# Dealing out PSUM in single-bank tiles in the first two phases of a transformer block's forward and backward pass

## Chip, cores, metric

One core of one Trainium2 chip. The metric is the device time of one execution in microseconds (us), the median of several runs. "The profile" is one profiled execution; its time axis starts with the span. Its records of matmuls can be a few per cent short, so counts of matmuls are rough.

## The reference, cut to what matters

A pre-layernorm block: attention over 8 keys at distance 0, 2, ... 14 (32 heads of 16), then an FFN with gelu, and the gradients of all of it for a given `grad_out`. S = 2048 tokens, D = 512, F = 1792, bf16.

```python
h  = x + attention(layernorm(x), wqkv, wo)      # 8 keys per token, dilation 2
h2 = h + gelu(layernorm(h) @ w1 + b1) @ w2 + b2
out, vjp = jax.vjp(h2_of, x, wqkv, wo, w1, b1, w2, b2)
return out, *vjp(grad_out)
```

## The kernel before

Three phases. Phase 1 is the attention forward pass by chunks of 512 tokens. Phase 2 is the FFN forward and backward, also by chunks. A handover joins them, in which chunk 3 finishes its attention while the FFN of chunk 0 starts. Phase 3 is the attention backward pass with the weight gradients. Instructions of phases 1 and 2 are put in order by a scheduler when the kernel is built, those of phase 3 by hand. These are the parts that the change and the argument touch:

```python
psY = pool("psY", 2, space=PSUM)       # 2 banks: Y(name) = one bank, 512 fp32
psT = pool("psT", 2, space=PSUM)       # 2 banks: transpositions
psX = pool("psX", 2, space=PSUM)       # 2 pairs of banks
def X(name):
    return psX.tile([P, 2, 512], F32, name=name, tag="x")
# ... phase 1: q, k, v and logits in X; ps_sum, ps_r, ps_wo and ps_band in Y

def p2_h(c):                           # first FFN matmul and gelu, chunk c
    for (f0, f1) in FB:                # blocks of 4, 4, 4, 2 slices of F
        # ... xb, xa: rings of 2 buffers
        for fp in range(f0, f1, 2):
            ps = X("ps_h")
            for i in range(2):
                # ... 4 matmuls into ps[:, i, :]
                A.activation(out=xb[...], in_=ps[:, i, :], func=ACT.Identity, bias=...)
                A.activation(out=x2[...], in_=ps[:, i, :], func=ACT.Square, bias=...)   # x2 is in xa
        gt, dt_ = block_tiles()        # ring of 5 blocks
        # ... eight DVE steps on xb, xa: gt = gelu, the last writes dt_ = gelu'
        tok_store(gt, f0, f1, gT_d, c) # transposition by DMA (SP queue), then a store (POOL)

def p2_rest(c):
    goT = ft("goT")
    SY.dma_start_transpose(out=goT[:], in_=gof[c * CH:(c + 1) * CH, :])
    # ...
    for j in range(TPC):               # FFN output: 16 matmuls per tile, read by ACT
        ps = Y("ps_f2")
    for bi, (f0, f1) in enumerate(FB):
        for fp in range(f0, f1, 2):
            ps = X("ps_gg")
            for i in range(2):
                # ... 4 matmuls w2T x goT into ps[:, i, :]
                # DVE: dt *= ps[:, i, :], with row sums (gb1p)
        tok_store(dts[bi], f0, f1, ghT_d, c)
    for j in range(TPC):               # gradient of the layernorm's output, read by ACT
        ps = Y("ps_gl2")
# ...
ms = tc.manual_schedule()              # phase 3 from here
ms.__enter__()
V.memset(glf[:, :, S:SP], 0.0)
```

A round of phase 2 has two parts. In the *section*, PE runs the 56 ps_gg matmuls of chunk c, its 56 ps_gl2 matmuls and some ps_h of chunk c+1. In the *FFN-output half*, it runs ps_f2 and the other ps_h of chunk c+1.

Of the kernel before, what the change touches and what calls it, by code (L numbers as in the profile page):

```python
# [36 lines left out]
def kernel(  # L37
# [57 lines left out]
    psX = pool("psX", 2, space=bass.MemoryType.PSUM)  # L95

    def X(name):
        return psX.tile([P, 2, 512], F32, name=name, tag="x")
# [157 lines left out]
    def dots(wp, ql, kw_, L, mask):  # L256
        for g in range(4):
            pr = wp.tile([P, W, 512], BF16, name="pr", tag="prod", bufs=2 + (wp is not late))
            V.tensor_tensor(out=pr[:], in0=ql[:, g, :].unsqueeze(1).to_broadcast([P, W, 512]),  # L259
                            in1=_sub(kw_[:, g, PAD:PAD + 512], [[-DIL, W], [1, 512]]), op=ALU.mult)  # L260
            for hf in range(2):
                for w4 in range(4):
                    T.matmul(L[32 * w4:32 * w4 + 32, hf, :], lhsT=Emat[:, g, :], rhs=pr[:, 2 * w4 + hf, :],
                             start=(g == 0), stop=(g == 3), skip_group_check=True)
        if mask:
            for hf in range(2):
                T.matmul(L[:, hf, 0:16], lhsT=mk[:, hf].rearrange("p a b -> p (a b)"), rhs=ident[0:16, 0:16],
                         start=False, stop=True, skip_group_check=True)
# [97 lines left out]
    def p1_proj(c, sel, dst, off):  # L366
        for g2 in range(2):
            ps = X("ps_qkv")
            for gg in range(2):
                g = 2 * g2 + gg  # L370
                for dc in range(DC):
                    T.matmul(ps[:, gg, :], lhsT=wqkv[:, dc, sel * D + g * P:sel * D + (g + 1) * P],  # L372
                             rhs=st_[c]["ln1T"][:, dc, :], start=(dc == 0), stop=(dc == DC - 1))
            A.copy(out=dst[:, 2 * g2:2 * g2 + 2, off:off + CH], in_=ps[:])  # L374
# [25 lines left out]
    def p1_dots(c):  # L400
        d = st_[c]
        d["L"] = X("ps_L")
        dots(late, d["qt"], d["kt"], d["L"], c == 0)

    def p1_sm1(c):
# [3 lines left out]
        A.copy(out=asb[:], in_=L[:, 0, :])  # L409
        m1 = late.tile([P, 512], BF16, name="m1", tag="m1", bufs=1)  # L410
        V.tensor_tensor(out=m1[:], in0=asb[:], in1=L[:, 1, :], op=ALU.max)
# [8 lines left out]
        for hf in range(2):  # L420
            T.matmul(L[:, hf, :], lhsT=nSum4[0:32, :], rhs=m3[:], start=False, stop=True, skip_group_check=True)
        e = late.tile([P, 2, 512], BF16, name="e", tag="e", bufs=1)
        A.activation(out=e[:], in_=L[:], func=ACT.Exp, scale=scale)
        d["e"] = e

    def p1_sm2(c):
        e = st_[c]["e"]
        pss = Y("ps_sum")
# [7 lines left out]
        psr = Y("ps_r")  # L436
# [23 lines left out]
    def p1_d(c):  # L460
        d = st_[c]
        oT, xt = d["oT"], d["xt"]
        ht = htile(f"h{c}")
        for j in range(TPC):
            ps = Y("ps_wo")
            for k in range(DC):
                T.matmul(ps[:], lhsT=oT[:, k, j * P:(j + 1) * P], rhs=wo[:, k, :], start=(k == 0), stop=False)
            T.matmul(ps[:], lhsT=ident[:], rhs=xt[:, j, :], start=False, stop=True)
            A.copy(out=ht[:, j, :], in_=ps[:])
        h_all.append(ht)  # L470
        ln2 = late.tile([P, TPC, D], BF16, name="ln2", tag="ln2", bufs=1)
        layernorm(late, ht, rstd2, c, ln2)
        store_rows(ln2_d, c, ln2)
        to_fm(ln2, ln2T[c])
# [84 lines left out]
    def p2_h(c):  # L559
        d = ps2[c]  # L560
        d["g"], d["d"] = [], []
        for (f0, f1) in FB:
# [4 lines left out]
            for fp in range(f0, f1, 2):  # L567
                ps = X("ps_h")
                for i in range(2):
                    f = fp + i  # L570
                    for dc in range(DC):
                        T.matmul(ps[:, i, :], lhsT=wcol(w1, dc, f), rhs=ln2T[c][:, dc, :],  # L572
                                 start=(dc == 0), stop=(dc == DC - 1))
                    A.activation(out=xb[:, f - f0, :], in_=ps[:, i, :], func=ACT.Identity, bias=b1c[:, f:f + 1])  # L574
                    A.activation(out=x2[:, f - f0, :], in_=ps[:, i, :], func=ACT.Square, bias=b1c[:, f:f + 1])  # L575
# [16 lines left out]
    def p2_rest(c):  # L592
# [8 lines left out]
        for j in range(TPC):  # L601
            ps = Y("ps_f2")
# [8 lines left out]
        for bi, (f0, f1) in enumerate(FB):  # L611
            for fp in range(f0, f1, 2):
                ps = X("ps_gg")
                for i in range(2):
                    f = fp + i
                    for dc in range(DC):
                        T.matmul(ps[:, i, :], lhsT=wcol(w2T, dc, f), rhs=goT[:, dc, :],  # L617
                                 start=(dc == 0), stop=(dc == DC - 1))
                    dsl = dts[bi][:, f - f0, :]
                    V.tensor_tensor_reduce(out=dsl, in0=ps[:, i, :], in1=dsl, scale=1.0, scalar=0.0,  # L620
# [5 lines left out]
        for j in range(TPC):  # L626
            ps = Y("ps_gl2")
# [31 lines left out]
    def p3_pre():  # L659
# [9 lines left out]
        L = X("ps_ga0")  # L669
        for g in range(4):  # L670
            pr = ft("xa", "pr0")
            ga_prod(pr[:].rearrange("p a b n -> p (a b) n"), got, vw, g)
            ga_sum(L, lambda w, pr=pr: pr[:, w // 4, w % 4, :], g)
# [3 lines left out]
        V.tensor_tensor(out=pp, in0=L[:], in1=attn_c(0), op=ALU.mult)  # L677
        ga_rows(L, pp)
        yield
        V.tensor_tensor(out=glf[:, :, 0:CH], in0=L[:], in1=attn_c(0), op=ALU.mult)  # L680
# [98 lines left out]

    V.memset(glf[:, :, S:SP], 0.0)  # L780
# [283 lines left out]
    for c in range(NC + 2):  # L1064
# [47 lines left out]
        if 0 < c < NC:  # L1112
            V.tensor_tensor(out=glf[:, :, c * CH:(c + 1) * CH], in0=L[:], in1=attn_c(c), op=ALU.mult)
        if c < NC:
# [83 lines left out]
```

## Time and profile before

726.1 us, median of 3 runs (723.9 to 727.1); the profiled execution had a span of 728.5 us. PE was busy for 85% of it, DVE 71%, ACT 51%. These are its milestones, read from the timelines of PE, DVE and SP (us from the span's start):

| milestone | before |
|---|---|
| last ps_wo of chunk 2 (end of phase 1) | 139.0 |
| woT issued on the SP queue | 184.1 |
| first ps_gg of chunk 0 (end of the handover) | 215.9 |
| sections of chunks 0, 1, 2 | 35.9, 35.0, 35.0 |
| FFN-output halves of chunks 1, 2, 3 | 26.1, 27.6, 17.7 |
| first ps_gg of chunk 3 to phase 3's first product | 47.3 |
| phase 3 from its first product on | 288 |

A section here runs from the first ps_gg to the end of the last ps_gl2, a half from there to the next ps_gg. The prediction shows most of the lines behind this table. Two more, which it names but does not show, are from the FFN-output half of chunk 2. Columns: start, duration, engine, line, operation, tiles, shapes, count, and in brackets the idle time before and what ended it. First the DVE timeline, then PE's.

```profile
311.10 1.22 DVE L586 TENSOR_TENSOR dt<-xa 128x2048 bf16<-128x2048 bf16 x1
314.87 1.23 DVE L586 TENSOR_TENSOR dt<-xa 128x2048 bf16<-128x2048 bf16 x1 [2.55 <-DMA tst<-dt]
```

```profile
314.17 1.67 PE L604 MATMUL ps_f<-w,gt 128*128 128x512 bf16 x7
318.51 1.86 PE L572 MATMUL ps_h<-ln2T,w 128*128 128x512 bf16 x4 [2.66 <-ACT xa L575]
```

DVE cannot write a new dt until the old one in that buffer has been transposed by DMA. xa and xb come free only with that step, ACT cannot empty ps_h before, and PE waits for ACT.

### The profile page before, as it was taken

The numbers are of one execution on the slowest core, as the hardware profiler recorded it, in microseconds if no ns is written. First come the engines' busy times: TensorE is split into PE (matmuls) and PEld (weight loads), VectorE is DVE, ScalarE is ACT, GpSimd is POOL, SyncE is SP. The second block draws the span as 40 slices with busy tenths as digits, with TensorE's granted clock in tenths as the row PEclk, the third lists the DMA queues.
The fourth block names the chain that finished last, engine by engine and source line by source line (L and its number), as shares of the span: only waits on it lengthen the run. The fifth ranks groups of instructions, "written<-read, shape, count | busy, mean of one in ns | idle before, by whom it ended". The sixth has DMA issues, their size and how long they took to land. (4 is left out here: it accounts for less than half of the span.)

```text
span 728.5 us, 10165 instructions
## 1 busy us (share of the span) xinstructions
PE 620.6 (85%) x3885; PEld 289.2 (40%) x3948; DVE 516.0 (71%) x756; ACT 368.7 (51%) x548; POOL 143.9 (20%) x183
## 2 busy tenths in 40 slices
PE   3887888658678988988889797989998999898997
PEld 1433343323223333333333332434444666543443
DVE  7869879479746886676694398987797798478400
ACT  1676686757643364555251235276358437463311
POOL 5222433322101010010001112122032124112100
PEclk9999999989799999999999998999999999999999
DMA  8772747714997696396489969977488869989341
GB/s 279 246 262 69 254 129 250 248 57 102 223 248 193 114 252 133 99 256 187 116 173 261 276 216 332 335 252 285 181 303 321 331 207 301 361 274 282 118 156 44
DMA packets 147806, 158.87 MB, mean 218 GB/s; under 512 B 94461, under 2 KB 132398, under 8 KB 141102
## 3 DMA queue, kind: packets, MB, share of 16 engines
q1 hardware_dynamic: 120078, 69.58, 37.2%
q0 software_dynamic: 15376, 77.63, 30.5%
q10 hardware_dynamic: 12304, 11.01, 4.8%
q8 instruction: 31, 0.51, 0.3%
q14 instruction: 17, 0.14, 0.1%
HBM read 87.63 MB, written 48.03 MB: 186 GB/s over the span
## 5 line engine op out<-in xcount | busy, mean ns | idle before, releaser
L982 DVE TENSOR_TENSOR prb<-R,cf 128x2048 bf16<-128x2048 bf16 x96 | 111.4, 1220 | 13.3 <-PE ps_band L990 7.1
L572 PE MATMUL ps_h<-ln2T,w 128*128 128x512 bf16 x220 | 62.1, 398 | 18.1 <-ACT xa L575 13.8
L620 DVE CUSTOM_DVE_ANT_0 dt<-ps_gg,dt 128x512 bf16<-128x512 f32 x56 | 37.9, 689 | 51.2 <-PE ps_gg L617 51.2
L617 PE MATMUL ps_gg<-goT,w2T 128*128 128x512 bf16 x218 | 55.2, 386 | 13.0 <-DVE gb1p L620 6.5
L574 ACT ACTIVATE xb<-ps_h,b1c 128x512 bf16<-128x512 f32 x56 | 38.5, 690 | 50.0 <-PE ps_h L572 49.3
L604 PE MATMUL ps_f<-w,gt 128*128 128x512 bf16 x218 | 54.8, 390 | 2.9 <-DVE gt L581 2.6
L629 PE MATMUL ps_gl<-w1T,dt 128*128 128x512 bf16 x218 | 55.2, 388 | 1.1 <-ACT gyr L211 0.7
L874 PE MATMUL ps_gw<-gwm,ln_r 128*128 128x256 bf16 x448 | 53.9, 275 | 1.6 <-ACT gwst L793 1.0
L866 PE MATMUL ps_gw<-gout_r,gwm 128*128 128x512 bf16 x215 | 53.6, 392 | 1.0 <-issue 0.8
L211 ACT ACTIVATE gyr<-ps_gl,rstd 128x512 bf16<-128x512 f32 x32 | 21.9, 687 | 63.7 <-PE ps_gl L1046 32.0
L372 PE MATMUL ps_qkv<-ln1T,wqkv 128*128 128x512 bf16 x185 | 47.2, 389 | 6.7 <-ACT kt L374 2.1
L874 PEld LDWEIGHTS <-ln_r 128*128 128x128 bf16 x448 | 42.8, 98 | 13.9 <-issue 6.9
L642 DVE TENSOR_TENSOR pr<-got,vw 128x4096 bf16<-128x4096 bf16 x16 | 36.5, 2289 | 14.7 <-DMA vw<-vf_d 9.2
L557 POOL DMA_DIRECT2D gT_d<-tst x16 | 12.0, 748 | 174.9 <-DMA tst<-gt 172.5
L894 PE MATMUL ps_gwq<-gqh,ln_r 128*128 128x512 bf16 x188 | 42.2, 379 | 1.5 <-DMA ln_r<-ln_d 1.3
L572 PEld LDWEIGHTS <-w 128*128 128x128 bf16 x224 | 22.0, 100 | 50.3 <-issue 32.7
L990 PE MATMUL ps_band<-prb,S 128*32 128x512 bf16 x384 | 31.8, 402 | 11.7 <-DVE prb L982 6.2
L580 ACT ACTIVATE xa<-xa 128x2048 bf16<-128x2048 bf16 (+1 forms) x16 | 27.2, 1698 | 28.4 <-DVE xa L579 28.4
L575 ACT ACTIVATE xa<-ps_h,b1c 128x512 bf16<-128x512 f32 x56 | 38.2, 689 | 2.5 <-DVE dt L586 2.5
L617 PEld LDWEIGHTS <-w2T 128*128 128x128 bf16 x224 | 21.9, 98 | 44.0 <-issue 21.8
L289 DVE TENSOR_TENSOR prb<-R,cf 128x2048 bf16<-128x2048 bf16 x32 | 37.5, 1209 | 2.6 <-PE ps_band L294 2.1
L259 DVE TENSOR_TENSOR pr<-qt,kt 128x4096 bf16<-128x4096 bf16 x16 | 35.9, 2283 | 4.1 <-ACT qt L374 2.6
(179 smaller groups left out, 1114.4 us busy)
## 6 DMA issues: line engine op xcount, KB each, us to landing
gwm<-ghT_d SPq DMA_DIRECT2D x7, 1024.0 KB
gT_d<-tst POOLq DMA_DIRECT2D x12, 512.0 KB
ghT_d<-tst POOLq DMA_DIRECT2D x12, 512.0 KB
gwm<-gT_d SPq DMA_DIRECT2D x6, 1024.0 KB
out_dram<-gwst ACTq DMA_DIRECT2D x22, 256.0 KB
ln_d<-ln POOLq DMA_DIRECT2D x8, 512.0 KB
vw<-vf_d SPq DMA_DIRECT2D x4, 528.0 KB
xt<-in_A_x_dram SPq DMA_DIRECT2D x4, 512.0 KB
```

Of the source, the lines that this page charges most:

```text
L372: T.matmul(ps[:, gg, :], lhsT=wqkv[:, dc, sel * D + g * P:sel * D + (g + 1) * P], rhs=st_[c]["ln1T"][:, dc, :], start=(dc == 0), stop=(dc ...
L572: T.matmul(ps[:, i, :], lhsT=wcol(w1, dc, f), rhs=ln2T[c][:, dc, :], start=(dc == 0), stop=(dc == DC - 1))
L574: A.activation(out=xb[:, f - f0, :], in_=ps[:, i, :], func=ACT.Identity, bias=b1c[:, f:f + 1])
L575: A.activation(out=x2[:, f - f0, :], in_=ps[:, i, :], func=ACT.Square, bias=b1c[:, f:f + 1])
L604: T.matmul(ps[:], lhsT=gts[f // 4][:, f % 4, j * P:(j + 1) * P], rhs=wrow(w2, f), start=(f == 0), stop=False)
L617: T.matmul(ps[:, i, :], lhsT=wcol(w2T, dc, f), rhs=goT[:, dc, :], start=(dc == 0), stop=(dc == DC - 1))
L620: V.tensor_tensor_reduce(out=dsl, in0=ps[:, i, :], in1=dsl, scale=1.0, scalar=0.0, op0=ALU.mult, op1=ALU.add, accum_out=gb1p[:, f, c:c + 1])
L629: T.matmul(ps[:], lhsT=dts[f // 4][:, f % 4, j * P:(j + 1) * P], rhs=wrow(w1T, f), start=(f == 0), stop=(f == FT - 1))
L866: yield from mm_pair("ps_gw2", lambda ps, o, u, i, t, k: T.matmul(ps[:], lhsT=g_[:, o, i * HN + t, :], rhs=gout_r[i][:, t, :], **k), MM, w ...
L874: yield from mm_pair("ps_gw1", lambda ps, o, u, i, t, k: T.matmul(ps[:, 256 * u:256 * u + 256].rearrange("p (a f) -> p a f", a=2), lhsT=ln ...
L894: yield from mm_pair("ps_gwq", lambda ps, o, u, i, t, k: T.matmul(ps[:], lhsT=ln1_r[i][:, t, (2 * d2 + o) * P:(2 * d2 + o + 1) * P], rhs=h ...
L982: V.tensor_tensor(out=pr[:, 4 * hf:4 * hf + 4].rearrange("p j (d h) -> p j d h", h=H), in0=R[:, o:o + 4, :].rearrange("p j (d h) -> p j d ...
```

## The change

PSUM is dealt out anew. X becomes four single banks instead of two pairs. ps_gg gets the two Y banks for itself, ps_f2 and ps_gl2 move into the transposition banks, and phase 1's ps_sum, ps_r and ps_wo move from Y to X. The intent is that each bank comes free by itself, and that ps_h (read by ACT) and ps_gg (read by DVE) no longer wait for each other. ps_ga0, the first product of phase 3's preparation, becomes two single tiles in the same way. The memset of glf's pad moves into phase 3. The diff, cut to its core:

```diff
-    psX = pool("psX", 2, space=bass.MemoryType.PSUM)
+    psX = pool("psX", 4, space=bass.MemoryType.PSUM)
-        return psX.tile([P, 2, 512], F32, name=name, tag="x")
+        return psX.tile([P, 512], F32, name=name, tag="x")
@@ phase 1: q, k, v; the logits likewise become a list of two tiles
-        for g2 in range(2):
+        for g in range(4):
             ps = X("ps_qkv")
...
-            A.copy(out=dst[:, 2 * g2:2 * g2 + 2, off:off + CH], in_=ps[:])
+            A.copy(out=dst[:, g, off:off + CH], in_=ps[:])
-        pss = Y("ps_sum")
+        pss = X("ps_sum")
-        psr = Y("ps_r")
+        psr = X("ps_r")
-            ps = Y("ps_wo")
+            ps = X("ps_wo")
@@ phase 2
-                ps = X("ps_h")
                 for i in range(2):
                     f = fp + i
+                    ps = X("ps_h")
...
-            ps = Y("ps_f2")
+            ps = psT.tile([P, 512], F32, name="ps_f2", tag="t")
-                ps = X("ps_gg")
                 for i in range(2):
                     f = fp + i
+                    ps = Y("ps_gg")
...
-            ps = Y("ps_gl2")
+            ps = psT.tile([P, 512], F32, name="ps_gl2", tag="t")
@@ phase 3
-    V.memset(glf[:, :, S:SP], 0.0)
...
+            if c == 1:
+                V.memset(glf[:, :, S:SP], 0.0)
```

More of the change, by code (lines that the diff above doesn't have):

```diff
@@ L262, in dots @@
                 for w4 in range(4):
-                    T.matmul(L[32 * w4:32 * w4 + 32, hf, :], lhsT=Emat[:, g, :], rhs=pr[:, 2 * w4 + hf, :],
+                    T.matmul(L[hf][32 * w4:32 * w4 + 32, :], lhsT=Emat[:, g, :], rhs=pr[:, 2 * w4 + hf, :],
                              start=(g == 0), stop=(g == 3), skip_group_check=True)
@@ L266, in dots @@
             for hf in range(2):
-                T.matmul(L[:, hf, 0:16], lhsT=mk[:, hf].rearrange("p a b -> p (a b)"), rhs=ident[0:16, 0:16],
+                T.matmul(L[hf][:, 0:16], lhsT=mk[:, hf].rearrange("p a b -> p (a b)"), rhs=ident[0:16, 0:16],
                          start=False, stop=True, skip_group_check=True)
@@ L366, in p1_proj @@
     def p1_proj(c, sel, dst, off):
-        for g2 in range(2):
+        for g in range(4):
             ps = X("ps_qkv")
-            for gg in range(2):
-                g = 2 * g2 + gg
-                for dc in range(DC):
-                    T.matmul(ps[:, gg, :], lhsT=wqkv[:, dc, sel * D + g * P:sel * D + (g + 1) * P],
-                             rhs=st_[c]["ln1T"][:, dc, :], start=(dc == 0), stop=(dc == DC - 1))
-            A.copy(out=dst[:, 2 * g2:2 * g2 + 2, off:off + CH], in_=ps[:])
+            for dc in range(DC):
+                T.matmul(ps[:], lhsT=wqkv[:, dc, sel * D + g * P:sel * D + (g + 1) * P],
+                         rhs=st_[c]["ln1T"][:, dc, :], start=(dc == 0), stop=(dc == DC - 1))
+            A.copy(out=dst[:, g, off:off + CH], in_=ps[:])
     def p1_qk(c):
@@ L401, in p1_dots @@
         d = st_[c]
-        d["L"] = X("ps_L")
+        d["L"] = [X("ps_L") for _ in range(2)]
         dots(late, d["qt"], d["kt"], d["L"], c == 0)
@@ L408, in p1_sm1 @@
         asb = late.tile([P, 512], BF16, name="asb", tag="asb", bufs=1)
-        A.copy(out=asb[:], in_=L[:, 0, :])
+        A.copy(out=asb[:], in_=L[0][:])
         m1 = late.tile([P, 512], BF16, name="m1", tag="m1", bufs=1)
-        V.tensor_tensor(out=m1[:], in0=asb[:], in1=L[:, 1, :], op=ALU.max)
+        V.tensor_tensor(out=m1[:], in0=asb[:], in1=L[1][:], op=ALU.max)
         m1h = late.tile([64, 512], BF16, name="m1h", tag="m1h", bufs=1)
@@ L420, in p1_sm1 @@
         for hf in range(2):
-            T.matmul(L[:, hf, :], lhsT=nSum4[0:32, :], rhs=m3[:], start=False, stop=True, skip_group_check=True)
+            T.matmul(L[hf][:], lhsT=nSum4[0:32, :], rhs=m3[:], start=False, stop=True, skip_group_check=True)
         e = late.tile([P, 2, 512], BF16, name="e", tag="e", bufs=1)
-        A.activation(out=e[:], in_=L[:], func=ACT.Exp, scale=scale)
+        for hf in range(2):
+            A.activation(out=e[:, hf, :], in_=L[hf][:], func=ACT.Exp, scale=scale)
         d["e"] = e
@@ L567, in p2_h @@
             for fp in range(f0, f1, 2):
-                ps = X("ps_h")
                 for i in range(2):
                     f = fp + i
+                    ps = X("ps_h")
                     for dc in range(DC):
-                        T.matmul(ps[:, i, :], lhsT=wcol(w1, dc, f), rhs=ln2T[c][:, dc, :],
-                                 start=(dc == 0), stop=(dc == DC - 1))
-                    A.activation(out=xb[:, f - f0, :], in_=ps[:, i, :], func=ACT.Identity, bias=b1c[:, f:f + 1])
-                    A.activation(out=x2[:, f - f0, :], in_=ps[:, i, :], func=ACT.Square, bias=b1c[:, f:f + 1])
+                        T.matmul(ps[:], lhsT=wcol(w1, dc, f), rhs=ln2T[c][:, dc, :], start=(dc == 0), stop=(dc == DC - 1))
+                    A.activation(out=xb[:, f - f0, :], in_=ps[:], func=ACT.Identity, bias=b1c[:, f:f + 1])
+                    A.activation(out=x2[:, f - f0, :], in_=ps[:], func=ACT.Square, bias=b1c[:, f:f + 1])
             gt, dt_ = block_tiles()
@@ L612, in p2_rest @@
             for fp in range(f0, f1, 2):
-                ps = X("ps_gg")
                 for i in range(2):
                     f = fp + i
+                    ps = Y("ps_gg")
                     for dc in range(DC):
-                        T.matmul(ps[:, i, :], lhsT=wcol(w2T, dc, f), rhs=goT[:, dc, :],
-                                 start=(dc == 0), stop=(dc == DC - 1))
+                        T.matmul(ps[:], lhsT=wcol(w2T, dc, f), rhs=goT[:, dc, :], start=(dc == 0), stop=(dc == DC - 1))
                     dsl = dts[bi][:, f - f0, :]
-                    V.tensor_tensor_reduce(out=dsl, in0=ps[:, i, :], in1=dsl, scale=1.0, scalar=0.0,
+                    V.tensor_tensor_reduce(out=dsl, in0=ps[:], in1=dsl, scale=1.0, scalar=0.0,
                                            op0=ALU.mult, op1=ALU.add, accum_out=gb1p[:, f, c:c + 1])
@@ L668, in p3_pre @@
         yield
-        L = X("ps_ga0")
+        L = [X("ps_ga0") for _ in range(2)]
         for g in range(4):
@@ L672, in p3_pre @@
             ga_prod(pr[:].rearrange("p a b n -> p (a b) n"), got, vw, g)
-            ga_sum(L, lambda w, pr=pr: pr[:, w // 4, w % 4, :], g)
+            for hf in range(2):
+                for w4 in range(4):
+                    w = 2 * w4 + hf
+                    T.matmul(L[hf][32 * w4:32 * w4 + 32, :], lhsT=Emat[:, g, :], rhs=pr[:, w // 4, w % 4, :],
+                             start=(g == 0), stop=(g == 3), skip_group_check=True)
             if g % 2:
@@ L676, in p3_pre @@
         pp = ft("tst", "pp0")[:, 0:8, :].rearrange("p (a b) f -> p a (b f)", a=2)
-        V.tensor_tensor(out=pp, in0=L[:], in1=attn_c(0), op=ALU.mult)
-        ga_rows(L, pp)
+        for hf in range(2):
+            V.tensor_tensor(out=pp[:, hf, :], in0=L[hf][:], in1=attn[:, hf, 0:CH], op=ALU.mult)
+        for hf in range(2):
+            for h2 in range(2):
+                T.matmul(L[hf][:], lhsT=nSum4[:], rhs=pp[:, h2, :], start=False, stop=(h2 == 1), skip_group_check=True)
         yield
-        V.tensor_tensor(out=glf[:, :, 0:CH], in0=L[:], in1=attn_c(0), op=ALU.mult)
+        for hf in range(2):
+            V.tensor_tensor(out=glf[:, hf, 0:CH], in0=L[hf][:], in1=attn[:, hf, 0:CH], op=ALU.mult)
     def run(g, n=1000):
```

## The prediction

> **What bounds the kernel now.** I read the page first, then the busy time by stretch, then the timelines of single engines. The kernel has three phases: attention forward (to 138 us), a handover that finishes chunk 3's attention and starts the FFN (138 to 216), FFN forward and backward by chunks of 512 tokens (to 435), and a hand-ordered third phase (to 728). This is the busy time by stretch; the columns are window, length, then busy time and count of PE, PEld, DVE, ACT and POOL, granted clock, DMA share, GB/s.
>
> ```profile
> core 0: us, PE busy (x) PEld busy (x) DVE busy (x) ACT busy (x) POOL busy (x), PEclk, DMA share, GB/s
> 60.00:138.00 78.00, 65.95 (x576) 31.86 (x584) 67.90 (x87) 59.66 (x77) 31.18 (x38) 1.00 0.58 186
> 138.00:216.00 78.00, 51.99 (x245) 21.00 (x249) 52.41 (x75) 49.37 (x70) 12.35 (x16) 0.87 0.70 174
> 252.00:278.00 26.00, 23.41 (x112) 10.03 (x113) 17.55 (x28) 15.64 (x26) 2.93 (x4) 1.00 1.09 226
> 278.00:313.00 35.00, 30.85 (x132) 12.94 (x135) 26.05 (x52) 13.80 (x23) 2.26 (x3) 1.00 0.53 110
> 393.20:435.00 41.80, 36.80 (x201) 15.83 (x204) 27.20 (x54) 11.22 (x23) 5.46 (x7) 0.96 0.83 250
> 435.00:728.00 293.00, 269.49 (x1916) 136.72 (x1941) 200.37 (x213) 139.76 (x220) 60.59 (x65) 0.98 0.74 257
> ```
>
> No engine is full in phase 1 (DVE 87%, PE 85%, ACT 76%): they wait in turn. The handover is the worst stretch: nobody is above 67%, and the clock is 0.87. An FFN round (252 to 313) is limited by PE with waits. The third phase the diff leaves as it is, but for one memset. Its first cause of loss in the handover is seen on the DVE timeline:
>
> ```profile
> 139.62 0.69 DVE L196 BATCH_NORM_STATS2 st<-h 128x6 f32<-128x512 bf16 x1 [0.41 <-ACT h L469]
> 148.63 0.18 DVE L197 BATCH_NORM_AGGREGATE mv<-st 128x2 f32<-128x6 f32 x1 [8.31 <-DMA q_d<-tmst]
> 148.63 0.07 DVE L780 MEMSET glf<- 128x16 uint32 x1
> 148.93 2.36 DVE L289 TENSOR_TENSOR prb<-R,cf 128x2048 bf16<-128x2048 bf16 x2
> ```
>
> A statistics step cannot wait for the stores to q_d. The memset of glf's pad can: glf takes over memory of the released pool that staged those stores, and in the order of DVE the memset stands just before that step and carries waits on all eight hardware DMA lanes. It sits there although phase 3 alone needs it. PE is starved by the same wait:
>
> ```profile
> 140.93 1.75 PE L572 MATMUL ps_h<-ln2T,w 128*128 128x512 bf16 x5 [1.96 <-ACT xa L575]
> 150.20 0.62 PE L294 MATMUL ps_band<-prb,S 128*32 128x512 bf16 x4 [7.52 <-DVE prb L289]
> 215.88 4.31 PE L617 MATMUL ps_gg<-goT,w2T 128*128 128x512 bf16 x11 [4.07 <-DMA goT<-in_grad_out_dram]
> ```
>
> The last line is the end of the handover: the first ps_gg waits for goT. The DMA queue of SP, in time, shows why goT is late:
>
> ```profile
> 165.94 12.86 SPq L556 DMA_TRANSPOSE tst<-gt  x2
> 184.05 2.00 SPq L528 DMA_TRANSPOSE woT<-in_A_wo_dram  x1
> 186.56 9.51 SPq L698 DMA_TRANSPOSE w2T<-in_B_w_dram  x3
> 196.12 8.87 SPq L700 DMA_TRANSPOSE w1T<-in_B_w_dram  x4
> 205.09 4.82 SPq L556 DMA_TRANSPOSE tst<-gt  x2
> 210.02 2.02 SPq L596 DMA_TRANSPOSE goT<-in_grad_out_dram  x1
> ```
>
> woT takes over the buffer of ln2T of chunk 0, so it waits for the last ps_h matmul of chunk 0 (PE ran it from 182.99 to 183.8). All else stands behind it in one queue: from there to the first ps_gg it is a fixed chain of 215.88 - 184.05 = 31.8 us.
>
> In the rounds, ps_h and ps_gg share two pair tiles of two banks, and a pair comes free only when both halves are read. PE timeline of chunk 1's ps_gg section:
>
> ```profile
> 282.81 1.89 PE L617 MATMUL ps_gg<-goT,w2T 128*128 128x512 bf16 x8 [1.41 <-DVE gb1p L620]
> 287.76 1.02 PE L617 MATMUL ps_gg<-goT,w2T 128*128 128x512 bf16 x4 [0.89 <-DVE gb1p L620]
> 289.57 0.81 PE L572 MATMUL ps_h<-ln2T,w 128*128 128x512 bf16 x3 [0.36 <-DVE gb1p L620]
> 295.19 1.02 PE L617 MATMUL ps_gg<-goT,w2T 128*128 128x512 bf16 x3 [0.49 <-ACT xa L575]
> 302.89 0.81 PE L572 MATMUL ps_h<-ln2T,w 128*128 128x512 bf16 x3 [0.46 <-DVE gb1p L620]
> ```
>
> ps_gg waits for ACT's reads of ps_h, and ps_h for DVE's reads of ps_gg: what separate tiles would end.
>
> **What the Trainium skill says.** "PSUM — Partial Sum Buffer", section "The four PSUM rules": one matmul's output is at most one bank of 512 fp32 values. So a pair tile is never needed by a matmul; it only ties two banks' release together. The waits above agree. "Perfetto Trace Analysis", section "Matmuls": independent groups should rotate through banks so that reading one overlaps the next group; that is the change's intent. Its section "Optimizing Scalar/DVE Operations" says each instruction pays a fixed access cost, so halving an evacuation adds one. The trace: 1024 columns take ACT 1.02 us (0.91 in a row), 512 take 0.59 (some 0.49 in a row), so two halves cost about 0.07 to 0.16 more. "TensorE: Matmul & The Clock Gate", Part 1: the clock is full or half, and half after an idle window of about 3.4 us. Here four matmuls take 1.89 us at 150.75, after the 7.5 us gap, and 1.02 when warm: it agrees.
>
> **The change, part by part.**
>
> *Memset moved out of the handover.* Removed: 0.07 us and its wait. Built, the changed kernel has no instruction on DVE's path there that waits for the last q_d stores; the first gelu step waits only for lanes of the v and first k store. What ends the wait then is the gathered R of chunk 3. The trace's DMA landings put it at 144.5 us against 148.63: 4.1 us saved on DVE, and no full 7.5 us gap on PE. In the new order the band products also stand in front of the layernorm. Walking DVE forward with the durations of the trace: fourth band product, ln2, ACT's table load and first sigmoid, first gt at about 159.5 (before 164.65); block 1's gt at 170 (before 175.49).
>
> *ps_h alone in four single banks.* Chunk 0's last two ps_h tiles need two banks, which come free as soon as ACT has read the first two of block 2, about 171 to 172; before, they stood in PE's order behind pairs until 183. So woT is then bound by the transpose of block 1's gt in front of it (170 + 1.2 + 2.1, about 173.4). That is 10.6 us earlier, and the fixed chain brings goT at 173.4 + 31.8 = 205.2. Is anything else later than that? DVE finishes the first gelu block of chunk 1 at about 201 (before 209.3), PE the FFN output of chunk 0 by about 197. So: handover 10.7 us shorter.
>
> *ps_gg in its own two banks, ps_h in four, ps_f2 and ps_gl2 in the transposition banks.* Eight warm matmuls take 1.89 us and four 1.02, so one costs (1.89 - 1.02) / 4 = 0.216 us. A ps_gg section has 56 ps_gg, 56 ps_gl2, 24 ps_h: 136 x 0.216 = 29.4 us, against 277.92 to 312.95 = 35.0 now. Walking the new order: each ps_gg tile takes PE 0.86 and DVE 0.62, between gelu steps of 0.60 and 1.14 to 1.22; with two banks PE catches up with DVE three or four times, by 0.2 to 0.5 us. That gives 30.5: 4.5 us saved, in three sections (chunk 3 has no ps_h, its section runs with gaps of 0.16 to 0.25 on DVE already) = 13.5. The FFN-output half of the round, 26.0 and 27.5 us now, loses its wait of 2.2 to 2.6 us of DVE for the DMA of dt (the dt products are ready earlier, the stores have time) and of PE for ACT after it; but DMA share is 1.09 there, so I count 1 us each, two rounds: 2. The last half (375.7 to 393.2, a wait of 1.83): 0.5.
>
> *End of phase 2.* From the first ps_gg of chunk 3 (393.25) the path goes over vw's load, which lands at 416.9, behind three transposes of dt in the SP queue; that order stays. Gain 0.
>
> *Phase 1.* Single tiles for q, k, v end waits of PE such as 1.10 us for ACT kt or vt (three), and ps_r no longer holds a band bank (1.40, 1.42, 0.61 us behind ACT rb). But the logits now hold two of four X banks for most of a chunk, and q, k, v, sums, ps_r and ps_wo share the rest. ACT pays 24 + 4 extra instructions of 0.07 to 0.16, 2 to 4 us at 76% load. Together: 2 us gained, with a wide margin.
>
> Sum: 10.7 + 13.5 + 2 + 0.5 + 2 = 28.7 us. Nobody's walk by hand finds every wait in a new order, so I take a sixth off: 24 us, and 726 - 24 = 702 us.
>
> **The rivals.** (1) *DVE takes over as the bound.* Two banks for ps_gg against two pairs before: if gelu steps stand in front of its reads, PE waits up to 1.2 us for each of 14 tiles. DVE's own sum, 17.55 + 26.05 = 43.6 us of 61, speaks against it; for it, the DVE queue is in order. It would halve the section gain: about 709. (2) *The DMA queue.* With a share of 1.09 in one half of each round and 0.53 in the other, shorter rounds may only run into the transposes; goT and the dt waits would then set the pace, and only the handover would remain: 726 - 12 = 714. (3) *Nothing but the memset counts*, because goT's chain hides the rest of the handover: 4 us there and the rounds, about 708. (4) *Phase 1 loses*: X's two free banks are shared by five kinds of tile, and ACT is later: 3 to 5 us given back.
>
> **Range and chances.** All rivals together would leave 5 to 10 us, none makes the kernel slower by itself; the full hand count, with 3 us more in the f halves, is 694. I predict 702, with 690 to 715 in 8 cases of 10. 2% faster is 711.6; that fails if rival 2 holds or two others together: 0.82 faster, 0.16 same, 0.02 slower.
>
> **What would show each step.** Right: no wait of DVE over 5 us near 140; woT issued near 173 and the first ps_gg near 204; ps_gg sections of 30 to 32 us; ps_h waits on DVE reads of ps_gg gone; the third phase still about 293 us. Wrong: woT still after 180; sections above 34 us with PE waiting for gb1p; DVE waits for tst<-dt longer than 3 us; first ps_h of phase 2 later than 122.6 (phase 1 lost); or a third phase that starts earlier and ends no sooner, waiting for data.

## The result, and the profile after

691.7 us, median of 4 runs (689.4 to 696.4), beside 726.6 us for the kernel before (723.9 to 728.6). The ratio is 0.953, with a 95% interval of 0.947 to 0.959. The profiled execution has a span of 689.4 us and a granted clock of 0.973 (before 728.5 and 0.969). The outputs are correct.

Busy time by stretch after the change: window, length, then busy time (and count) of PE, PEld, DVE, ACT and POOL, granted clock, DMA share, GB/s. The four rows are the section of chunk 0, the half of chunk 1, the section of chunk 1 and the half of chunk 2; below them stands the half of chunk 2 in the kernel before.

```profile
203.00:236.10 33.10, 32.80 (x137) 13.88 (x137) 27.25 (x56) 12.77 (x22) 3.84 (x5) 0.91 0.96 208
236.10:256.60 20.50, 20.12 (x89) 8.15 (x88) 15.52 (x25) 12.66 (x21) 2.94 (x4) 1.00 0.98 233
256.60:287.10 30.50, 30.43 (x138) 13.18 (x137) 26.94 (x56) 15.23 (x27) 3.02 (x4) 1.00 0.81 183
287.10:308.50 21.40, 21.40 (x97) 8.96 (x96) 15.76 (x25) 13.82 (x23) 2.94 (x4) 1.00 1.00 218
```

```profile
313.00:340.50 27.50, 23.74 (x95) 9.44 (x97) 17.53 (x28) 15.75 (x27) 4.45 (x6) 0.94 0.91 241
```

PE now fills the rounds. In the last of the four rows it is busy all the time, at full clock, where the same half took 27.6 us before. The next lines show why: first DVE around the start of that half, then PE. The two dt products run without a wait for tst<-dt, and ps_h runs 15 and 16 matmuls in a row without a wait for ACT.

```profile
285.74 2.36 DVE L584 TENSOR_TENSOR dt<-xa 128x2048 bf16<-128x2048 bf16 x2
```

```profile
287.13 3.40 PE L571 MATMUL ps_h<-ln2T,w 128*128 128x512 bf16 x15
...
305.01 3.62 PE L571 MATMUL ps_h<-ln2T,w 128*128 128x512 bf16 x16
308.46 1.89 PE L615 MATMUL ps_gg<-goT,w2T 128*128 128x512 bf16 x8
```

The handover after the change, on DVE, on the SP queue and on PE:

```profile
137.88 1.23 DVE L289 TENSOR_TENSOR prb<-R,cf 128x2048 bf16<-128x2048 bf16 x1 [5.61 <-DMA R<-v_d,rowi]
```

```profile
169.28 2.14 SPq L527 DMA_TRANSPOSE woT<-in_A_wo_dram  x1
171.93 10.86 SPq L703 DMA_TRANSPOSE w2T<-in_B_w_dram  x3
182.83 8.55 SPq L705 DMA_TRANSPOSE w1T<-in_B_w_dram  x4
191.50 5.29 SPq L555 DMA_TRANSPOSE tst<-gt  x2
196.89 1.98 SPq L594 DMA_TRANSPOSE goT<-in_grad_out_dram  x1
```

```profile
202.99 3.57 PE L615 MATMUL ps_gg<-goT,w2T 128*128 128x512 bf16 x8 [4.77 <-DMA goT<-in_grad_out_dram]
```

The band product that waited for the memset until 148.93 now runs at 137.88, and woT is issued 14.8 us earlier. The first ps_gg still waits for goT, and its eight matmuls take 3.57 us after the gap, 1.89 when warm. Where the 39.1 us between the two spans came from:

| part | before | after | gained | predicted |
|---|---|---|---|---|
| span's start to first ps_gg | 215.9 | 203.0 | 12.9 | 12.7 (phase 1: 2, handover: 10.7) |
| three sections | 106.0 | 94.6 | 11.4 | 13.5 |
| three FFN-output halves | 71.4 | 56.4 | 14.9 | 2.5 |
| end of phase 2 | 47.3 | 45.4 | 1.9 | 0 |
| phase 3 | 288.0 | 290.0 | -2.0 | 0 |

The parts add up to 39.1; differences were taken before rounding. The medians differ by less, 34.9 us: the profiled execution of the kernel before was one of its slower ones. Phase 3 has the same instructions in nearly all kernels, but takes between 285 and 295 us in their profiles, so its -2.0 means nothing. Part of the halves' 14.9 is work that only moved. The 16 PE transpositions of gh of chunk 0 went from the half of chunk 1 to the end of phase 2 (1.06 us). And the three halves hold 54 ps_h matmuls on record where they held 70: the sections have 9 more (75 and 66), the rest runs before the first ps_gg. At 0.216 us each these 16 are an estimated 3.5 us. So some 4.5 of the 14.9 us are moved, and about 10 are waits, and what came with them, that ended; the sections gained their 11.4 us although they took on about 2 us of ps_h.

### The profile page after: what moved, and what is told of

The parts are those of the page before. It is cut to its first block, busy times and chain, and to the rows that moved or that the text cites. A ratio compares the mean times of both kernels' runs of the same rounds, so it can differ in the third digit from the quotient of the medians.

```text
span 689.4 us, 10271 instructions
## 1 busy us (share of the span) xinstructions
PE 621.6 (90%) x3948; PEld 291.2 (42%) x3948; DVE 513.0 (74%) x758; ACT 368.7 (53%) x576; POOL 148.7 (22%) x183
## 5 line engine op out<-in xcount | busy, mean ns | idle before, releaser
L571 PE MATMUL ps_h<-ln2T,w 128*128 128x512 bf16 x224 | 58.4, 395 | 1.5 <-ACT xa L573 0.8
L617 DVE CUSTOM_DVE_ANT_0 dt<-ps_gg,dt 128x512 bf16<-128x512 f32 x56 | 38.0, 686 | 27.3 <-PE ps_gg L615 27.3
L211 ACT ACTIVATE gyr<-ps_gl,rstd 128x512 bf16<-128x512 f32 x32 | 22.0, 687 | 65.8 <-PE ps_gl L626 30.7
L626 PE MATMUL ps_gl<-w1T,dt 128*128 128x512 bf16 x224 | 52.9, 379 | 1.9 <-ACT tmst L240 1.1
L602 PE MATMUL ps_f<-w,gt 128*128 128x512 bf16 x224 | 51.6, 380 | 0.4 <-DVE gt L579 0.4
L639 DVE TENSOR_TENSOR pr<-got,vw 128x4096 bf16<-128x4096 bf16 x16 | 36.3, 2289 | 16.0 <-DMA vw<-vf_d 10.7
L993 PE MATMUL ps_band<-prb,S 128*32 128x512 bf16 x384 | 31.1, 390 | 10.7 <-ACT got L636 5.1
L995 ACT ACTIVATE gks<-ps_band 128x512 bf16<-128x512 f32 x32 | 19.0, 598 | 36.4 <-PE ps_band L993 31.4
L240 ACT COPY tmst<-ptm 128x1024 bf16<-128x1024 bf16 x32 | 31.4, 1020 | 12.2 <-PE ptm L237 5.9
L259 DVE TENSOR_TENSOR pr<-qt,kt 128x4096 bf16<-128x4096 bf16 x16 | 35.9, 2279 | 1.5 <-PE ps_band L294 1.0
```

The lines of the kernel that those rows point to most:

```text
L571: T.matmul(ps[:], lhsT=wcol(w1, dc, f), rhs=ln2T[c][:, dc, :], start=(dc == 0), stop=(dc == DC - 1))
L602: T.matmul(ps[:], lhsT=gts[f // 4][:, f % 4, j * P:(j + 1) * P], rhs=wrow(w2, f), start=(f == 0), stop=False)
L617: V.tensor_tensor_reduce(out=dsl, in0=ps[:], in1=dsl, scale=1.0, scalar=0.0, op0=ALU.mult, op1=ALU.add, accum_out=gb1p[:, f, c:c + 1])
L626: T.matmul(ps[:], lhsT=dts[f // 4][:, f % 4, j * P:(j + 1) * P], rhs=wrow(w1T, f), start=(f == 0), stop=(f == FT - 1))
```

## The experiments

My theory was that of the prediction: the memset and the pairs each hold part of the handover, and in the rounds ps_h and ps_gg, read by different engines, must not share tiles (theory A). The rivals: the memset makes the whole handover; single banks alone are enough (B); or other waits take over. This table has all runs; "rounds" is first ps_gg of chunk 0 to first ps_gg of chunk 3. While PE waits for a late first ps_gg, more of chunk 1's ps_h can get done before it, so differences of 1 to 2 us in this column mean little.

| run | median us | ratio to before (95%) | woT issued | first ps_gg | rounds |
|---|---|---|---|---|---|
| before | 726.6 | 1 | 184.1 | 215.9 | 177.4 |
| changed kernel | 691.7 | 0.953 (0.947 to 0.959) | 169.3 | 203.0 | 151.0 |
| e1 memset only | 724.5 | 0.992 (0.986 to 0.998) | 178.7 | 210.5 | 177.6 |
| e2 memset back | 694.4 | 0.949 (0.942 to 0.957) | 168.5 | 201.0 | 149.9 |
| e3 own pools, pairs | 701.6 | 0.963 (0.956 to 0.970) | 178.6 | 209.7 | 156.1 |
| e4 singles, shared | 692.0 | 0.950 (0.945 to 0.955) | 170.5 | 208.6 | 151.2 |
| e5 before, dt plain | 715.8 | 0.984 (0.977 to 0.990) | 184.9 | 216.4 | 169.2 |
| e6 ps_gg in X | 690.3 | 0.949 (0.943 to 0.955) | 168.9 | 204.9 | 150.4 |
| e7 phase 1 in Y | 696.7 | 0.960 (0.952 to 0.968) | 169.7 | 210.4 | 148.8 |
| e8 preparation early | 695.6 | 0.955 (0.948 to 0.962) | 170.0 | 206.2 | 156.8 |
| e9 changed, again | 690.9 | 0.951 (0.948 to 0.953) | 168.1 | 200.7 | 151.2 |
| e10 goT first | 687.5 | 0.946 (0.943 to 0.948) | 169.1 | 195.8 | 151.7 |
| e11 goT first, vw early | 682.4 | 0.941 (0.937 to 0.944) | 169.7 | 196.5 | 151.5 |

### e1: the memset alone

```diff
 (kernel before)
-    V.memset(glf[:, :, S:SP], 0.0)
+            if c == 1:
+                V.memset(glf[:, :, S:SP], 0.0)
```

> The kernel before, with only the memset of glf's pad moved into the third phase; all PSUM pools as before. Theory A (as predicted, the memset's wait and the pairs each hold part of the handover): the DVE wait of 8.31 us shrinks by about 4, woT is still tied to pairs and issues at 178 to 181 (before 184.05, after 169.28), sections stay at 35 us, f halves at 26 to 27.5: 720 to 723 us. Rival B (the memset is all of the handover's gain): woT near 170 to 174 and 715 to 718 us. Rival C (other waits take its place): no change, 725 to 727.

Measured: 724.5 us (719.2 to 725.3), 0.8% faster than the kernel before in the same rounds (median 729.4), a little above the 720 to 723 expected. The DVE timeline where the memset stood:

```profile
143.32 2.36 DVE L289 TENSOR_TENSOR prb<-R,cf 128x2048 bf16<-128x2048 bf16 x2 [1.98 <-DMA R<-v_d,rowi]
```

The product starts 5.6 us earlier than at 148.93, because R's landing ends the wait. First gt at 159.2 us (predicted for this step: 159.5), woT at 178.7, first ps_gg 5.4 us earlier. Theory A holds here, the memset is not the whole handover: woT stays 9 us later than in the changed kernel. Sections (35.9, 35.0, 35.0) and halves (27.3, 26.8, 17.6) are as before.

### e2: the changed kernel with the memset put back

The reverse of that edit, on the changed kernel.

> The changed kernel with the memset put back at the end of the program's second phase, pools as changed. Theory A: 4 to 6 us of the 35 come back: 695 to 698 us, sections still 30.5 us and f halves 20.5 to 21.5. Rival B (the memset is all of the handover's gain): 700 to 702 us. Rival C: 690 to 693, nothing comes back, because the memset's wait is hidden once ps_h has four banks.

Measured: 694.4 us (685.9 to 695.6). This median lies between the ranges of C and of A and decides nothing; the ratio, 0.949 beside the changed kernel's 0.953, and the wait speak for rival C. The memset in DVE's order, in this run:

```profile
144.35 0.07 DVE L785 MEMSET glf<- 128x16 uint32 x1 [0.45 <-DMA q_d<-tmst]
```

It waits 0.45 us instead of 8.31. In the new order four band products stand ahead of it (137.21 to 143.8), and the last q_d stores have landed in the meantime. So what the memset cost depended on its place in DVE's order, and with the new PSUM layout its move gains nothing that these runs resolve.

### e3: own pools, but pairs for ps_h

```diff
 (kernel before, memset moved; phase 1 as before; ps_h still a pair)
-            ps = Y("ps_f2")
+            ps = psT.tile([P, 512], F32, name="ps_f2", tag="t")
-                ps = X("ps_gg")
+                    ps = Y("ps_gg")        # one per slice
-            ps = Y("ps_gl2")
+            ps = psT.tile([P, 512], F32, name="ps_gl2", tag="t")
```

> The kernel before with the memset moved, ps_gg in the two Y banks and ps_f2 and ps_gl2 in the transposition banks as in the changed kernel, but ps_h still in pairs, and phase 1 in its old pools. If the gain of the sections and the f halves comes from separating ps_h from ps_gg (theory A): sections 30.5 to 31.5, f halves 21 to 22.5, and what is lost against the changed kernel is phase 1 (3 us) and some of the handover: 695 to 700 us. If it comes from single banks (rival B): sections 33 to 35, f halves 25 to 27, and 712 to 720 us.

Measured: 701.6 us (697.4 to 705.1), a little above theory A's 695 to 700. Sections 34.6, 32.6, 32.6; halves 20.2, 20.2, 15.9. The sections are longer than A expected, since the scheduler put more ps_h into them (88 matmuls on record in the three, 75 in the changed kernel) and fewer into the halves; only the length of the rounds compares. Separation alone gives 21.3 of the 26.4 us gained in the rounds. It does nothing for woT (178.6, like e1), which still waits for chunk 0's last ps_h.

### e4: single banks, but shared as before

```diff
 (changed kernel)
-            ps = psT.tile([P, 512], F32, name="ps_f2", tag="t")
+            ps = Y("ps_f2")
-                    ps = Y("ps_gg")
+                    ps = X("ps_gg")
-            ps = psT.tile([P, 512], F32, name="ps_gl2", tag="t")
+            ps = Y("ps_gl2")
```

> The changed kernel with ps_h and ps_gg sharing the four X banks, one bank a tile, and ps_f2 and ps_gl2 back in the Y banks: single tiles as in the changed kernel, the phase-2 pools as before. Theory A (separate pools): ps_gg waits for ACT and ps_h for DVE again, sections 33 to 35, f halves 24 to 27: 708 to 716 us. Rival B (single banks): within 1% of the changed kernel, 690 to 695 us.

Measured: 692.0 us (690.9 to 694.5). Theory A expected 708 to 716 and falls; rival B is right. Sections 32.4, 29.8, 29.8; halves 21.4, 22.5, 15.4. With before, e3 and the changed kernel this makes a square, by the length of the rounds: pairs shared 177.4, pairs apart 156.1, singles shared 151.2, singles apart 151.0. Either step ends the waits of ps_h and ps_gg for each other, single banks do it fully, and separation on top adds nothing. ps_h and ps_gg share four banks in e4, as they did before: what was costly was not sharing, but sharing in units that come free only as a whole.

The waits before this run's first ps_gg, from the PE timeline:

```profile
208.58 0.59 PE L615 MATMUL ps_gg<-goT,w2T 128*128 128x512 bf16 x1 [10.59 <-DMA goT<-in_grad_out_dram]
```

woT was nearly as early as in the changed kernel, but 38.1 us lie between it and the first ps_gg, not 33.7: w2T alone held the queue for 13.84 us (10.86 there).

The half of chunk 2 shows one thing more. DVE's wait for tst<-dt is still there, but now costs PE less. DVE, then PE:

```profile
293.85 1.23 DVE L584 TENSOR_TENSOR dt<-xa 128x2048 bf16<-128x2048 bf16 x1 [2.02 <-DMA tst<-dt]
```

```profile
299.13 0.60 PE L602 MATMUL ps_f<-w,gt 128*128 128x512 bf16 x2 [0.92 <-DVE gt L579]
```

With four single banks PE runs 16 ps_h and 12 ps_f matmuls without a stop from 292.00 on, so a wait of 2.02 us on DVE costs PE 0.92 us and no slow matmul. In the kernel before one of 2.55 us cost 2.66 us and the slow matmuls after it. e6 shows the same (2.22 and 1.12 us).

### e5: no transposition of dt, in the kernel before

The clean test of the dt wait would be a sixth block of gt and dt. I took it not to fit in SBUF, and no run tried it. So the transposition is left out instead, and what depends on the stored dt is wrong.

```diff
 (kernel before; the w1 gradient is wrong on purpose)
-            tok_store(dts[bi], f0, f1, ghT_d, c)
+            G.dma_start(out=ghT_d[:, f0:f1, c, :], in_=dts[bi][:, 0:f1 - f0, :])
```

> The kernel before with the transposition of dt left out: dt is stored as it lies, so two outputs are wrong on purpose. It takes 16 transposing transfers of 2 to 4 us out of the SP queue and with them DVE's wait for tst<-dt. Theory A (what the FFN-output halves lost was that wait, passed on to ACT and PE and followed by matmuls at half clock): the halves of chunks 1 and 2, 26.0 and 27.6 us, fall to 21 to 24 though the pools are as before; sections stay at 34 to 35 us, since the pairs still bind there; total 712 to 720. Rival B (the pairs hold PE in the halves too): halves stay at 25 to 27, total 720 to 727.

One output was wrong, the w1 gradient, not two as expected. Measured: 715.8 us (714.9 to 717.9). Sections 35.3, 35.0, 35.0, unmoved; halves 23.8, 23.9, 16.1, together 7.6 us shorter. The PE timeline of the half of chunk 2:

```profile
313.51 1.02 PE L572 MATMUL ps_h<-ln2T,w 128*128 128x512 bf16 x4
...
332.11 2.18 PE L572 MATMUL ps_h<-ln2T,w 128*128 128x512 bf16 x8 [0.63 <-ACT xa L575]
```

The gap of 2.66 us and the slow matmuls after it are gone with the dt wait, under the old pools. So the chain from the transposition over DVE and ACT to PE is shown, and worth half of what the halves gained: 6.3 us less of idle PE and 1.3 us less of matmuls at half clock. The halves hold the same matmuls as before (70 ps_h on record), so nothing of this is moved work. The run also takes load off the queue, so it does not tell a dt product that is ready earlier from a queue that is emptier. Its total gained more than its halves, because the end of phase 2 is shorter too (42.5 us, 47.3 before): DVE can use vw 4.2 us after its issue, 7.3 before.

Of the other half (14.9 - 7.6 = 7.3), about 4.5 us are the moved work named above. What is left, some 3 us, is put down to the shared pairs by difference only: PE still idles for 2.3 us in this run's three halves, half of it for ACT's reads of ps_h as in the last line above, and for 0.9 us in the changed kernel's.

### e6: ps_gg in X, ps_f2 and ps_gl2 in the transposition banks

```diff
 (changed kernel)
-                    ps = Y("ps_gg")
+                    ps = X("ps_gg")
```

> The changed kernel with ps_gg moved from its own two banks into the four X banks beside ps_h; ps_f2 and ps_gl2 stay in the transposition banks, so the Y banks lie idle in most of the second phase. After the run with shared single banks, theory B (one bank a tile is enough, whoever shares) expects rounds of 52 to 54 us, the same as the changed kernel, 688 to 694 us, and an earlier first ps_gg than that run's 208.6 if its late one came from ps_f2 in the Y banks. Rival (own banks for ps_gg matter): rounds of 56 us and more, 698 us or more.

Measured: 690.3 us (690.1 to 691.5); rounds of 52.9, 52.4 and 45.0 us. It confirms e4: own banks for ps_gg do not matter here. The first ps_gg is indeed earlier than e4's, at 204.9, but it still waits 9.04 us for goT.

### e7: phase 1's sums and output projection back in Y

```diff
 (changed kernel)
-        pss = X("ps_sum")
+        pss = Y("ps_sum")
-        psr = X("ps_r")
+        psr = Y("ps_r")
-            ps = X("ps_wo")
+            ps = Y("ps_wo")
```

> The changed kernel with ps_sum, ps_r and ps_wo of the first phase back in the two Y banks (beside the band sums); q, k, v and logits stay as single tiles. If moving these three made the first phase shorter, its end (the last ps_wo of chunk 2, 135.7 us; before 139.0) goes back by 1 to 3 us and the total rises to 692 to 695. If the single tiles for q, k and v did it: no change there and a total of 690 to 692.

Measured: 696.7 us (695.8 to 703.5), with the last ps_wo of chunk 2 at 135.1 (changed kernel 135.7). The total rises, as the first reading expected, but not for its reason: phase 1 ends no later. By exclusion, the 3.3 us that phase 1 gained come from the other part of its change, the single tiles for q, k, v and the logits; these were not tried by themselves. The loss is on the SP queue, where the scheduler now put a third transposition of gt ahead of goT, and where goT itself held the queue for 4.73 us instead of 1.98:

```profile
193.60 7.54 SPq L555 DMA_TRANSPOSE tst<-gt  x3
201.25 4.73 SPq L594 DMA_TRANSPOSE goT<-in_grad_out_dram  x1
```

The first ps_gg comes at 210.4, 7.4 us later than in the changed kernel, though woT was issued at the same time.

### e8: phase 3's preparation ahead of chunk 3's ps_gg

```diff
 (changed kernel; in the loop over chunk 3's steps, behind ps_f2)
+                pre = p3_pre()
+                run(pre, 1)      # transposes gh of chunk 0, go, issues vw; go's stores stay behind
```

> The changed kernel with the first step of the third phase's preparation (transposing gh of chunk 0, go, the load of vw) put ahead of chunk 3's ps_gg section instead of after it. The DVE wait of 10.7 us for vw should go: vw is issued near 346 to 360 instead of 372.5, its products run between the ps_gg reads, and the stretch from the first ps_gg of chunk 3 to the third phase shrinks from 45.7 to 38 to 41 us (PE is busy 40.6 of it, some of this moves ahead): 684 to 688 us. Rival: the third phase then waits for data that other transfers bring (gathered k rows) and the total stays at 690 to 692.

Measured: 695.6 us (693.0 to 698.8), slower than the changed kernel. vw was issued 9 us earlier and DVE's wait for it shrank to 0.70 us. But the section became longer: DVE's products of 2.29 us each stand between its reads of ps_gg, so the 56 ps_gg take from 363.0 to 383.3 us instead of 12.8. Then ACT waits, and PE behind it, first on ACT's timeline and then on PE's:

```profile
388.94 1.01 ACT L240 COPY tmst<-ptm 128x1024 bf16<-128x1024 bf16 x1 [5.68 <-DMA ghT_d<-tst]
```

```profile
390.01 7.52 PE L626 MATMUL ps_gl<-w1T,dt 128*128 128x512 bf16 x28 [3.52 <-ACT tmst L240]
```

ACT's copy into tmst takes its buffer from the ring tst, so it waits until a transposed dt has been stored from there. From chunk 3's first ps_f2 to phase 3 it is 67.5 us instead of 60.5. Taking one wait away there made two others.

### e9, e10, e11: the two waits that remain

e9 is the changed kernel again, for comparison in the same rounds.

> The changed kernel as it is, timed once more beside the next two runs so that they can be compared with it and not only with the kernel before: 689 to 694 us, with the first ps_gg at 201 to 206 us after the span's start and waiting 4 to 6 us for goT, and DVE waiting 10 to 11 us for vw after the last ps_gg.

Measured: 690.9 us (686.2 to 691.4); first ps_gg at 200.7 with 3.79 us of waiting, a little under the expected 4 to 6.

e10 puts goT of chunk 0 ahead of w2T in the queue:

```diff
 (changed kernel)
+    goT0 = ft("goT")
+    SY.dma_start_transpose(out=goT0[:], in_=gof[0:CH, :])
     for a_, b_, t_ in w2T:
         SY.dma_start_transpose(out=t_[:], in_=B_w2[a_ * P:b_ * P, :])
...
-        goT = ft("goT")
-        SY.dma_start_transpose(out=goT[:], in_=gof[c * CH:(c + 1) * CH, :])
+        goT = ft("goT") if c else goT0
+        if c:
+            SY.dma_start_transpose(out=goT[:], in_=gof[c * CH:(c + 1) * CH, :])
```

> The changed kernel with goT of chunk 0 put ahead of w2T and w1T in the SP queue (it stood behind them and two transposes of gt). In all runs so far the first ps_gg waited for goT, 3.6 to 10.6 us. If goT's place in the queue sets the end of the handover: no wait for goT, first ps_gg 5 to 7 us earlier (at 196 to 198; w2T lands near 186, PE is done with the FFN outputs of chunk 0 at 198), and it runs at full clock: 684 to 688 us. Rival: another transfer or DVE's gelu of chunk 1 takes its place, less than 2 us gained: 689 to 692 us.

Measured: 687.5 us (683.8 to 689.6), against e9 a ratio of 0.9455 / 0.9505 = 0.995. From the SP queue and the PE timeline:

```profile
171.75 2.87 SPq L704 DMA_TRANSPOSE goT<-in_grad_out_dram  x1
174.74 9.81 SPq L706 DMA_TRANSPOSE w2T<-in_B_w_dram  x3
```

```profile
195.83 1.89 PE L616 MATMUL ps_gg<-goT,w2T 128*128 128x512 bf16 x8
```

No wait, full clock, 4.9 us earlier than e9, just short of the 5 to 7 expected. The median moved by 3.4 us, within the range expected; the intervals of the two ratios (0.943 to 0.948 and 0.948 to 0.953) only just touch.

e11 adds a place of its own for phase 3's first vw. It was a ring buffer that ghT held until go was computed; now it is the two block tiles that chunk 3 leaves unused.

```diff
 (e10; called behind chunk 3's ps_f2)
+    def load_vw0():
+        for i, t_ in enumerate(block_tiles()):     # an unused gt and dt
+            v_ = # ... the tile's first 2 * (PAD + CH) columns as two slices
+            SY.dma_start(out=v_, in_=vf_d[:, 2 * i:2 * i + 2, 0:PAD + CH])
+            vw0.append(v_)
...
-        vw = ft("xb", "vw0")
-        SY.dma_start(out=vw[:], in_=vf_d[:, :, 0:PAD + CH])
```

> As the run with goT first, and vw of the third phase's preparation loaded into the two block tiles that chunk 3 leaves unused, right behind the FFN outputs of chunk 3 and ahead of the transposes of dt, instead of into the ring buffer that ghT holds. The DVE wait of 10.7 us for vw should shrink to the 4 to 5 us until got is there; from the first ps_gg of chunk 3 to the third phase 41 to 43 us instead of 45.7: another 3 to 4 us, 680 to 685 us. Rival: the transposes of dt or the third phase's gathers set that end, and it stays where the run before is.

Measured: 682.4 us (677.7 to 687.5), correct, ratio 0.941 to the kernel before; its interval (0.937 to 0.944) lies below e9's (0.948 to 0.953). On DVE:

```profile
364.47 4.49 DVE L676 TENSOR_TENSOR pr<-got,gt 128x4096 bf16<-128x4096 bf16 x2 [2.97 <-ACT got L637]
```

The wait for vw (10.68 us in the changed kernel, 10.24 in e10) became one of 2.97 us for got. The end of phase 2 takes 43.8 us (expected 41 to 43; e10: 45.6), so 1.8 us is shown of the 5.1 between the two medians. The profile of e10 has a third phase of 294.7 us and that of e11 one of 285.3. That is the spread of phase 3 named above, so how much of the 5.1 us is e11's own stays open.

## Why the prediction was right, and where it was not

The total is inside the range (690 to 715), but 10 us below the 702 predicted, near the range's lower end.

**The memset.** Its own step was right in the old order: first gt at 159.2 in e1, predicted 159.5. In the changed kernel R landed at 137.9, not at 144.5 as taken over from the old trace, because its gather was issued at 129.7 instead of 134.8. Even so DVE waits 5.61 us for it there, so the prediction's own sign of being right, "no wait of DVE over 5 us near 140", did not come true; the wait is for R now, not for the memset. And e2 shows that the memset no longer mattered there. The step's 4.1 us is a cost of the old order, not a term to add to the new one.

**woT and ps_h in single banks.** Right in mechanism. With pairs woT is issued at 178.6 and 178.7 (e1, e3), with single banks at 168.1 to 170.5 in all nine such profiles, behind the transposition of block 1's gt. Predicted was 173.4; all of the handover came 4 us earlier, most of it from phase 1.

**"A fixed chain of 215.88 - 184.05 = 31.8 us."** The chain was 33.7 us in the changed kernel and 31.1 to 40.7 in the others in which goT stood behind w1T. It is a queue that the scheduler orders anew each time, with transfers of varying length. The two errors partly cancelled, which is luck: woT was 4.1 us earlier and the chain 1.9 longer than predicted, so 205.2 predicted, 203.0 measured.

**Sections.** 30.5 predicted, 30.7 measured for chunks 1 and 2, though not for the reasons given. PE does not fall back on DVE by 0.2 to 0.5 us three or four times: it waits for DVE 0.06 us in all in chunk 1's section, which holds 138 matmuls where 136 were counted. (The 0.216 us of one matmul is its step in the trace; the quotient shown with it gives 0.2175.) Separate tiles for ps_h and ps_gg were not what it took: e4 and e6 share and have sections of 29.8. Chunk 0's section is 33.3, 2.6 longer, partly because it starts at half clock behind goT. In e10 it starts warm and is still 33.9: with goT that early, 32 ps_h matmuls fall into it instead of 25 (an estimated 1.5 us), and PE waits 1.4 us for ACT and DVE.

**FFN-output halves: the step that failed.** "but DMA share is 1.09 there, so I count 1 us each, two rounds: 2. The last half (375.7 to 393.2, a wait of 1.83): 0.5." Measured: 14.9, of which about 10 are waits that ended and 4.5 are moved work, which the prediction did not foresee either. The waits were named correctly, and a busy DMA queue was taken as a reason to discount them. After the change the share in these halves is 0.98 and 1.00, yet the wait is gone. In the section of chunk 1 the last transposition of dt before the half is issued 23.9 us after the section's start instead of 34.7. The DVE products come earlier (the twelfth ends at 19.0 us instead of 24.9), and the scheduler's new order has goT of the next chunk behind these transpositions, where it stood in front; the runs do not part the two. Also left out were the matmuls at half clock behind a gap and ACT's waits for ps_h pairs. The gap need not be as long as the 3.4 us that the prediction quotes: 2.66 us was followed by half clock in the kernel before and 2.22 us in e1, but not 2.30 us in the kernel before, nor 2.92 in e1.

**End of phase 2.** 0 predicted, 1.9 measured; vw's wait stayed (10.7 us), as said. **Phase 1.** 2 predicted, 3.3 measured. (Of the three waits listed as 1.10 us for kt or vt, one is in fact 1.28 us for qt.) The extra cost on ACT was there as predicted: its copies of q, k, v and its exponentials of the logits take 31.7 us instead of 28.4, with 28 more instructions. ACT's busy time in all stayed at 368.7 us, and phase 1 became shorter all the same. The sign named for a loss, "first ps_h of phase 2 later than 122.6", did come: 135.5 in the changed kernel. It was a bad sign: ps_h now starts behind the last ps_wo of chunk 2, and both phase 1 and the handover end earlier.

**The sixth taken off.** Without the halves' 2.5 the sum held 26.2 us, and the same parts gave 24.3. So the sum needed no deduction for waits overlooked; the deduction of 4.7 and the halves' 12.4 are the miss.

**The rivals.** DVE did not become the bound: in the rounds after, PE is the one that is busy, 97 to 100% of the time. The DMA queue did not pace the rounds, but it did set the end of the handover, and e10 shows what that was worth. "Nothing but the memset" is refuted by e1 (0.8%) and e2. Phase 1 did not lose. (The sentence that all rivals together would leave 5 to 10 us does not follow from their sizes: 24 less 7, 12, 6 and 3 to 5 leaves nothing.)

## What to carry to other kernels

Hand out PSUM in the unit that is written and read at once. A tile of two banks, shared in turn by two engines, makes each wait for the other's reads, and it does not take more banks or separate pools to end that: e4 did it with the same banks. When a wait is named in a chain, follow it to the first thing that is late, and count what it drags along (the next engine's wait, the clock after the gap) before discounting it for a busy queue. After such a change look again at who waits: here one transfer's place in a queue and one buffer's owner gave another 1% on top of the 5%.

## What the Trainium skill lacked or had wrong

- "Perfetto Trace Analysis", section "Matmul Optimizations", asks to use all eight PSUM banks. Here that was not what mattered. In the rounds e6 leaves the two Y banks without ps_gg, ps_f2 or ps_gl2 and takes 690.3 us, with a ratio of 0.949, where the changed kernel with all eight has 0.951 and 0.953.
- "PSUM — Partial Sum Buffer", section "The four PSUM rules", limits a matmul to one bank but does not say what a tile over two banks costs when, as in this kernel, its banks come free together. The rounds took 177.4 us with shared pairs and 151.2 us with single banks shared in the same way.
- "DMA: Bandwidth & Descriptors", section "Latency and other measured facts", gives 261 GB/s for a transposing DMA with a non-contiguous middle dimension. It does not say how long such a transfer holds the queue that issues it, nor how much that varies. Here the three transfers of w2T held the SP queue for 8.87 us in e3 and for 13.84 us in e4, and that helped to decide when goT came.
- No page says that the end of a wait can move with the order of the instructions alone: the same memset with the same wait on stores cost 8.31 us in one order and 0.45 us in another.
